# Weight decoding from groups of two chunks, and the first block's convolution in six pieces

## The chip, the cores and the metric

One core of a Trainium2 chip runs the whole kernel. The metric is the device time in microseconds (us). The engines are named as the profile names them: PE (TensorE; its weight loads are PEld), DVE (VectorE), ACT (ScalarE), POOL (GpSimd) and SP (SyncE, which issues the DMAs here).

## What is computed

```python
# x: (4, 4096, 192), weight_gen: (4, 4096, 8, 7); w_in: (192, 2048), w_out: (2048, 192)
w = softmax(weight_gen, axis=-1)                       # 7 weights per token and head
x_pad = concatenate([zeros((B, 6, D)), x], axis=1)
out[b, s, head h] = sum over k of w[b, s, h, k] * x_pad[b, s + k, head h]
h = out.reshape(16384, 192) @ w_in
g = where(h >= 1, h, where(h <= -1, 0, (h + 1)**2 / 4))
return (g @ w_out).astype(float32)
```

The two weight matrices arrive as 64-bit floats, because a float32 array is multiplied by a float64 scalar. The kernel turns them into 32-bit numbers itself; this is called decoding below.

## The kernel before

**Blocks and pairs.** The 16384 tokens are cut into 32 blocks of 512. For each block the 2048 hidden features are worked through in 16 steps of 128, two steps at a time: a pair. There are 8 pairs per block (NP) and 256 in all. A pair is 18 matmuls of the first product (`gemm1_pair`, L378, high and low parts of x and of the weights), then per step a relu pass, a square pass (ACT, L389 and L392), a min/max pass (DVE, L397, `act_g`), a high part (ACT, L403) and a low part (DVE, L404, `gl`), then 32 matmuls of the second product (`gemm2_part`, L432), which come two pairs later. The order of instructions on each engine is the order in which the code is written; each engine works its list in order.

**Decoding.** The weights come in 8 chunks (NCH) of two steps each; chunk c serves pair c. Part 0 of a chunk is its piece of w_in, part 1 its piece of w_out, each 128 partitions by 384 numbers. For each part a pass takes the top 16 bits of every 64-bit number into `head` (`cast_act` on ACT, L327; `cast_dve` on DVE, L331), a DVE pass joins them with the lower bits (`merge`, L340, two inputs in SBUF, result `psw` in a PSUM bank), and a high and a low part are written to `whi`/`wlo` or `wo` (`high` on ACT, L352; `low` on DVE, L356). All 64-bit numbers that a pass reads lie 8 bytes apart. Chunks 0 to 2 are decoded at the start and in `first_pairs`; chunk c = w + 1 is decoded during pair w in `early_pair`, for w = 2 to 6. From block 1 on no decoding is left.

**Block 0.** DVE and POOL form products of x with one of the 7 weights of the convolution, as pieces (`alone`, L227): one on DVE and three on POOL, and DVE adds three further products into a fifth (L244). PE turns each piece into the layout of the first product, four 128x128 turns for each third of the 192 features (`turn_sum`, L267, 60 turns in all), and sums the pieces in PSUM as it turns them. The last third also reads features 0 to 63 again, which `again` (ACT, L169) copies behind each piece. ACT and DVE then write the high and low parts `hc` and `hl` (L258, L259).

**Later blocks.** POOL does the whole convolution (L179 products, L189 sums). Block 1's result is turned on PE in pair 7 (`turn1`, `edge_pair`); from block 2 on DVE turns 32x32 squares (L284) and DMAs do the rest, and POOL writes the low parts `hl`. POOL's operations for block 1 wait by hand-made dependencies for the latest decoding pass of DVE (`gate`, `marks`). `ps_h` has 4 PSUM banks, shared by x, by decoded weights and by pairs.

**Loads.** SP issues them in this order: weight_gen, block 0's x, chunks 0, 1 and 2, block 1's x, chunk 3; the first chunk's load waits for a softmax pass of DVE. A chunk's rows are 1 KB (w_in) and 1.5 KB (w_out).

Of the kernel before, what the change touches and what calls it, by code (L numbers as in the profile page):

```python
# [22 lines left out]
def kernel(  # L23
# [21 lines left out]
    nc = tc.nc  # L45
# [38 lines left out]
    raw = ctx.enter_context(tc.tile_pool(name="raw", bufs=4))  # L84
# [131 lines left out]
    def conv_summed(b):  # L216
# [30 lines left out]
        return alone, wn, wt[:, gi], lambda: times(nc.vector, acc, wn, 1), add, own  # L247
# [4 lines left out]
    def split_x(b, src, engines):  # L252
# [8 lines left out]
        return ops  # L261

# [41 lines left out]
    def load_weights(c, behind=None):  # L304
        r = raw.tile([P, 4 * CN + 2], U16, tag="r", name="r")
        for h in range(2):
            f = c * CF + h
            load = nc.sync.dma_start(
                out=r[h * Q:(h + 1) * Q, 1:1 + 4 * C1].rearrange("q (k c) -> q k c", k=NC),
                in_=w_in[:, f * P:(f + 1) * P].rearrange("(k q) c -> q k c", q=Q).bitcast(U16))  # L310
            if behind is not None:
                tc.add_manual_dep(load.ins, behind.ins.name, SYNC, reason="the first block goes first")
                behind = None
# [18 lines left out]

    psw = {}

    def merge(c, part):
        word = raw_t[c].bitcast(U32)[:, 1:1 + 2 * CN].rearrange("p (c t) -> p c t", t=2)[:, :, 0]
# [423 lines left out]
```

## Time and profile before

| | |
|---|---|
| device time, 3 runs | median 1143.42 us (1143.4 to 1144.77) |
| span of the profiled execution | 1141.3 us (first to last instruction; no other time of that execution is given, so the median lies 2.1 us above the span) |
| PE busy | 1128.6 us (99%) |
| ACT, DVE, POOL busy | 964.6, 833.6, 792.3 us (85, 73, 69%) |
| granted PE clock | 1.000 over the span (the upper of the two levels) |
| DMA | 91.43 MB; busiest in the first 38 us |

Times are counted from the first instruction. A busy PE is not a PE at its peak, since matmuls are pipelined and their ends modelled: the count of matmuls in a stretch says more than the busy share.

### The profile page before, as it was taken

To read this page: it belongs to the slowest core of one execution; us is meant where nothing else is said; L and a number is where in the kernel's file an instruction comes from. 1 tells how busy PE (TensorE), PEld (TensorE's weight loads), DVE (VectorE), ACT (ScalarE), POOL (GpSimd) and SP (SyncE) were. 2 spreads that over 40 slices of the span, in tenths; PEclk is the share of its full clock that TensorE was granted. 3 is DMA by queue.
4 is the path that set the end of the run, shared out by engine and by line. 5 is a ranking of instruction groups with operands and counts; after the bars stand their busy time and mean duration, and the time that the engine had idled before them with its cause. 6 is when DMAs were issued, how large, how long until landed. Compare 5 with 4: busy or idle time off the path is not lost.

```text
span 1141.3 us, 32240 instructions
## 1 busy us (share of the span) xinstructions
PE 1128.6 (99%) x12885; PEld 1077.9 (94%) x12885; DVE 833.6 (73%) x1271; ACT 964.6 (85%) x1745; POOL 792.3 (69%) x511
## 2 busy tenths in 40 slices
PE   7999999999999999999999999999999999999998
PEld 5789999999999999999999999999999999999998
DVE  8877867777676777767777676776767777677765
ACT  6878888888888888888888888888888888888886
POOL 4799876777857678586686866678586785866310
PEclk9999999999999999999999999999999999999999
DMA  9422222222222212222122222222222122221100
GB/s 228 118 67 82 92 86 92 77 65 74 90 78 91 69 65 90 81 87 91 43 90 73 85 92 78 65 74 90 77 92 76 57 91 82 82 91 43 48 24 29
DMA packets 84053, 91.43 MB, mean 80 GB/s; under 512 B 5056, under 2 KB 75712, under 8 KB 83904
## 3 DMA queue, kind: packets, MB, share of 16 engines
q1 hardware_dynamic: 83904, 89.39, 24.7%
q8 instruction: 101, 1.65, 0.6%
q14 instruction: 48, 0.39, 0.1%
HBM read 64.99 MB, written 24.38 MB: 78 GB/s over the span
## 4 chain that ended last, share of the span: by engine, by line
PE 94%; ACT 3%; DVE 2%; issue 1%; DMA 0%; DVEq 0%; POOL 0%; POOLq 0%
PE o L432 47%; PE psh L378 46%; ACT u L392 1%; PE psx L267 1%; ACT gh L403 1%; DVE psh L397 1%; ACT u L389 1%; DMA x<-in_x_dram 0%; ACT whi L352 0%; DVE psw L340 0%; DVE gl L404 0%; ACT wo L352 0%; ACT osb L456 0%; DVE wo L356 0%; DVE piece L227 0%
## 5 line engine op out<-in xcount | busy, mean ns | idle before, releaser
L432 PE MATMUL o<-wo,gh 64*128 64x384 f32 x4096 | 645.5, 353 | 1.0 <-SPq L441 1.0
L432 PE MATMUL o<-wo,gl 64*128 64x192 f32 x4096 | 623.4, 247 | 0.0
L432 PEld LDWEIGHTS o<-wo,gh 64*128 64x128 f32 x4096 | 592.9, 184 | 6.5 <-SPq L441 1.2
L432 PEld LDWEIGHTS o<-wo,gl 64*128 64x128 f32 x4096 | 573.1, 187 | 0.1
L397 DVE SCALAR_TENSOR_TENSOR psh<-u,psh 128x512 f32<-128x512 f32 x512 | 354.4, 695 | 283.3 <-ACT u L392 282.9
L378 PE MATMUL psh<-hc,whi 64*128 64x512 f32 x1536 | 461.0, 395 | 4.2 <-DVE wlo L356 2.8
L378 PE MATMUL psh<-hc,wlo 64*128 64x512 f32 x1536 | 453.9, 389 | 0.0
L378 PE MATMUL psh<-hl,whi 64*128 64x512 f32 x1536 | 452.4, 388 | 0.0
L389 ACT ACTIVATE u<-psh 128x512 f32<-128x512 f32 x512 | 301.2, 588 | 78.2 <-PE psh L378 77.1
L404 DVE TENSOR_TENSOR gl<-psh,gh 128x512 fp32r<-128x512 f32 x512 | 345.5, 685 | 14.7 <-ACT gh L403 0.5
L403 ACT ACTIVATE gh<-psh 128x512 fp32r<-128x512 f32 x512 | 299.5, 592 | 63.4 <-DVE psh L397 63.4
L189 POOL TENSOR_TENSOR acc<-acc,pr 128x768 f32<-128x768 f32 x185 | 343.8, 1858 | 5.7 <-DVE head L331 2.0
L392 ACT ACTIVATE u<-u 128x512 f32<-128x512 f32 x512 | 324.3, 633 | 16.0
L378 PEld LDWEIGHTS psh<-hc,whi 64*128 64x128 f32 x1536 | 281.5, 184 | 19.3 <-DVE wlo L356 4.8
L378 PEld LDWEIGHTS psh<-hl,whi 64*128 64x128 f32 x1536 | 281.0, 184 | 15.7 <-DVE hl L259 0.3
L179 POOL TENSOR_TENSOR pr<-x,w 128x768 f32<-128x768 f32 x186 | 287.0, 1550 | 7.1 <-DVE psw L340 7.1
L378 PEld LDWEIGHTS psh<-hc,wlo 64*128 64x128 f32 x1536 | 282.0, 185 | 10.3
L259 POOL TENSOR_TENSOR hl<-XT,hc 128x512 fp32r<-128x512 f32 x90 | 115.6, 1297 | 206.9 <-PE o L432 151.6
L179 POOL TENSOR_TENSOR acc<-x,w 128x768 f32<-128x768 f32 x31 | 48.0, 1547 | 70.2 <-DVE w L155 68.3
L258 ACT ACTIVATE hc<-XT 128x512 fp32r<-128x512 f32 x90 | 55.5, 618 | 0.0
L284 DVE STREAM_TRANSPOSE T<-acc 128x768 f32<-128x768 f32 x30 | 50.0, 1665 | 0.0
L457 DVE SCALAR_TENSOR_TENSOR osb<-o,osb 128x384 f32<-128x384 f32 x64 | 32.5, 548 | 2.9 <-ACT osb L456 2.8
(44 smaller groups left out, 189.0 us busy)
## 6 DMA issues: line engine op xcount, KB each, us to landing
x<-in_x_dram SPq DMA_DIRECT2D x28, 960.0 KB, 4.8
XT<-D SPq DMA_DIRECT2D x180, 128.0 KB, 2.7
out_dram<-osb SPq DMA_DIRECT2D x31, 384.0 KB, 3.2
D<-T SPq DMA_DIRECT2D x30, 384.0 KB, 2.3
x<-in_x_dram SPq DMA_DIRECT2D x4, 945.0 KB
w<-in_weight_gen_dram SPq DMA_DIRECT2D x15, 224.0 KB, 2.6
r<-in_moe_w_in_dram SPq DMA_DIRECT2D x16, 192.0 KB, 7.1
r<-in_moe_w_out_dram SPq DMA_DIRECT2D x8, 384.0 KB, 12.3
```

The lines of the kernel that those rows point to most:

```text
L179: held(eng.tensor_tensor(out=t, in0=xtile[:, k:k + n, :].rearrange("p j (h g) -> p j h g", h=H), in1=wt[:, gi, :, :, k:k + 1].to_broadcast ...
L189: held(eng.tensor_tensor(out=o, in0=s, in1=t, op=ALU.add))
L258: ops.append(lambda c=c: nc.scalar.activation(out=hc[:, c], in_=src[c], func=AF.Copy))
L259: ops.append(lambda c=c: lows.append(engines[c].tensor_tensor(out=hl[:, c], in0=src[c], in1=hc[:, c].bitcast(F32), op=ALU.subtract)))
L284: lambda: nc.vector.transpose(out=T.rearrange("p b c j -> p b j c"), in_=acc.rearrange("p j (r b) -> p b j r", b=R)),
L378: nc.tensor.matmul(out=pair[h][:, 0:N], lhsT=l[rows, f // 2, (c + h) % NC if b < 2 else c], rhs=r[rows, c], start=(s == 0), stop=(s == len ...
L389: nc.scalar.activation(out=u_t[i], in_=h_t[i][:, 0:N], func=AF.Relu, scale=0.5 * UNIT, bias=0.5)
L392: nc.scalar.activation(out=u_t[i], in_=u_t[i], func=AF.Square, scale=UNIT ** -0.5)
L397: nc.vector.scalar_tensor_tensor(out=pv, in0=uv, scalar=1.0 / UNIT, in1=pv, op0=ALU.min, op1=ALU.max)
L403: nc.scalar.activation(out=gh[:, 0:N], in_=gv, func=AF.Copy)
L404: nc.vector.tensor_tensor(out=gl[:, 0:N], in0=gv, in1=gh[:, 0:N].bitcast(F32), op=ALU.subtract)
L432: mm = nc.tensor.matmul(out=o_t[b][turn][:, k, 0:cols], lhsT=g_t[i][l][rows, t * P:(t + 1) * P], rhs=wo[rows, f].rearrange("p s d -> p (s ...
```

## The change

Weights are loaded in groups of two chunks (rows of 2 and 3 KB). The two chunks of a group are the even and the odd columns of its part of w_in, and the even and odd rows of w_out. So a pass that reads part 0 of a chunk now finds its 64-bit numbers 16 bytes apart; in part 1 they stay 8 bytes apart. The load of the first group waits for nothing, and block 1's x is issued behind it. Block 0's convolution has six pieces: DVE makes two products alone and adds two into a third piece, POOL makes three. Each piece takes eight turns (48 in all), for two banks; the last third of `hc` is copied by ACT out of the two banks, 64 partitions each, and that of `hl` by POOL out of the other thirds. The same holds for block 1. Casts move between DVE, ACT and POOL, and `first_pairs` is in another order, with its end in `second_pair`.

```diff
-    raw = ctx.enter_context(tc.tile_pool(name="raw", bufs=4))
+    raw = ctx.enter_context(tc.tile_pool(name="raw", bufs=2))
...
-        return alone, wn, wt[:, gi], lambda: times(nc.vector, acc, wn, 1), add, own
+        return alone, wn, wt[:, gi], lambda: times(nc.vector, acc, wn, 2), add, own
...
+        def over(to, of, c):
+            nc.gpsimd.tensor_copy(out=hl[to, NC - 1], in_=hl[of, c])
+
+        return {
+            "hc0": lambda: high_of(hc[:, 0], src[0]), "hc1": lambda: high_of(hc[:, 1], src[1]),
+            "hcU": lambda: high_of(hc[upper, NC - 1], src[0][lower]),
+            "hcL": lambda: high_of(hc[lower, NC - 1], src[1][upper]),
+            "hl0": lambda: low_of(0), "hl1": lambda: low_of(1),
+            "hlU": lambda: over(upper, lower, 0), "hlL": lambda: over(lower, upper, 1)}
...
-            out=r[:, 1 + 4 * C1:1 + 4 * CN].rearrange("p (f c) -> p f c", f=CF),
-            in_=w_out[c * CF * P:(c + 1) * CF * P, :].rearrange("(f p) c -> p f c", p=P).bitcast(U16))
-        raw_t[c] = r
+            out=r[:, 1 + 8 * C1:1 + 8 * CN].rearrange("p (f c) -> p f c", f=CF),
+            in_=w_out[f0:f0 + 2 * CF * P, :].rearrange("(f p e) c -> p f (e c)", p=P, e=2).bitcast(U16))
+        raw_t[g] = r
+
+    def of_chunk(v, c, part):
+
+        if part == 0:
+            return v[:, 0:2 * C1].rearrange("p (k c e) -> p e k c", k=NC, e=2)[:, c % 2]
+        return v[:, 2 * C1:2 * CN].rearrange("p (f e d) -> p e f d", f=CF, e=2)[:, c % 2]
...
+        if w == 0:
+            passes = [p for p in passes if p[1] is hc] + [p for p in passes if p[1] is hl]
...
-        load_weights(0, marks[6])
+        load_weights(0)
+        load_x(1)
         load_weights(1)
-        load_weights(2)
-        load_x(1)
-        load_weights(3)
...
         cast_act(0, 0)
-        again(own[0])
-        pieces.append(own[0])
+        cast_act(1, 0)
+        cast_pool(0, 1)
...
         def first_pairs():
+            high(1, 0)
+            low(1, 0)
+            cast_act(1, 1)
             merge(0, 1)
             merge(1, 1)
...
+            wave(1)
+            load_weights(2)
+            gemm1_pair(1)
+            high(0, 1)
             relu(0)
...
+            cast_dve(2, 0)
             merge(2, 0)
...
+            wave(2)
...
+        def second_pair():
+            cast_dve(2, 1)
             split_g(2)
             split_g(3)
+            merge(2, 1)
+            high(2, 1)
             cast_act(3, 0)
+            low(2, 1)
             cast_dve(3, 1)
...
-            splits = split_x(1, src1, [nc.vector] * NC)
+            x1 = split_turned(1, src1)
...
-            turn1(2)
             gemm2_part(w - 1, 1)
             split_g(i)
+            x1["hcU"]()
+            x1["hcL"]()
+            x1["hlU"]()
+            x1["hlL"]()
```

DVE's list for block 0's sum, from the first piece to the first `merge`, before:

```order
L227 TENSOR_TENSOR piece_173<-x_111,near_154 128x4x192
L227 TENSOR_TENSOR sums_155<-x_111,near_154 128x768
L227 TENSOR_TENSOR tap_183<-x_111,near_154 128x768
L244 TENSOR_TENSOR sums_155<-sums_155,tap_183 128x768
L227 TENSOR_TENSOR tap_189<-x_111,near_154 128x768
L244 TENSOR_TENSOR piece_191<-sums_155,tap_189 128x4x192
L340 SCALAR_TENSOR_TENSOR psw_255<-r_135,head_99 128x384
```

and after the change:

```order
L224 TENSOR_TENSOR piece_164<-x_111,near_146 128x768
L224 TENSOR_TENSOR piece_168<-x_111,near_146 128x768
L224 TENSOR_TENSOR sums_147<-x_111,near_146 128x768
L224 TENSOR_TENSOR tap_175<-x_111,near_146 128x768
L240 TENSOR_TENSOR piece_177<-sums_147,tap_175 128x768
L369 SCALAR_TENSOR_TENSOR psw_230<-r_135,head_99 128x384
```

One of the two additions is gone, and the products go to two pieces instead of one.

DVE's list in the changed kernel from the two `merge` passes of w_out's chunks 0 and 1 to the last low part of pair 0 (`r_140` is the second group, `head_99` and `head_100` take even and odd chunks, `psh0_250` and `psh0_251` are pair 0):

```order
L369 SCALAR_TENSOR_TENSOR psw_273<-r_135,head_99 128x384
L369 SCALAR_TENSOR_TENSOR psw_275<-r_135,head_100 128x384
L386 TENSOR_TENSOR wo_98<-psw_273,wo_98 128x2x192
L356 TENSOR_SCALAR head_99<-r_140 128x384
L369 SCALAR_TENSOR_TENSOR psw_308<-r_140,head_99 128x384
L429 SCALAR_TENSOR_TENSOR psh0_250<-u_304,psh0_250 128x512
L386 TENSOR_TENSOR wlo_97<-psw_308,whi_96 128x384
L429 SCALAR_TENSOR_TENSOR psh0_251<-u_318,psh0_251 128x512
L386 TENSOR_TENSOR wo_98<-psw_275,wo_98 128x2x192
L436 TENSOR_TENSOR gl_325<-psh0_250,gh_324 128x512
L436 TENSOR_TENSOR gl_329<-psh0_251,gh_328 128x512
```

Chunk 2's first cast (the fourth row) stands on DVE right behind these merges and reads the second group; before, it stood on ACT, and both merges of chunk 2 came before the first min/max pass of pair 0. Now only one does.

POOL's list in the changed kernel around the end of block 1's convolution and the start of block 2's (`acc_788`):

```order
L186 TENSOR_TENSOR piece_249<-acc_277,pr_679 128x768
L176 TENSOR_TENSOR acc_788<-x_446,w_109 128x768
L176 TENSOR_TENSOR pr_790<-x_446,w_109 128x768
L273 COPY hl_841<-hl_841 64x512 x2
L176 TENSOR_TENSOR pr_920<-x_446,w_109 128x768
L186 TENSOR_TENSOR acc_788<-acc_788,pr_790 128x768
```

The two copies of `hl` are new in this list; they stand behind the second product of block 2, and the rest of that convolution stands behind them.

## Rows read from the trace of the kernel before

**Rows 1.** Busy time by stretch: us, each engine's busy (instructions), clock, DMA, GB/s.

```profile
12.80:28.20 15.40, 11.99 (x98) 9.03 (x98) 14.60 (x30) 12.47 (x25) 5.52 (x4) 1.00 1.09 253
28.20:50.20 22.00, 20.54 (x209) 17.24 (x208) 20.61 (x40) 19.18 (x39) 13.59 (x8) 1.00 0.66 155
80.60:1100.00 1019.40, 1019.40 (x11776) 983.58 (x11778) 740.20 (x1115) 875.67 (x1578) 736.28 (x469) 1.00 0.24 78
```

**Rows 2.** Timeline of block 0's start: start, duration, instruction, idle before and releaser.

```profile
7.20 0.95 DVE L227 TENSOR_TENSOR piece<-x,near 128x768 f32<-128x768 f32 x1 [0.28 <-DMA x<-in_x_dram]
8.21 6.77 PE L267 MATMUL psx<-ident,piece 128*128 128x128 f32 x60 [0.22 <-DVE piece L227]
14.14 1.58 ACT L258 ACTIVATE hc<-psx 128x512 fp32r<-128x512 f32 x3 [0.25 <-PE psx L267]
```

**Rows 3.** Timeline, DVE: the merges of chunks 3, 4 and 7.

```profile
28.19 1.03 DVE L340 SCALAR_TENSOR_TENSOR psw<-r,head 128x384 uint32<-128x384 uint32 x2
...
33.41 1.02 DVE L340 SCALAR_TENSOR_TENSOR psw<-r,head 128x384 uint32<-128x384 uint32 x2
...
49.09 1.02 DVE L340 SCALAR_TENSOR_TENSOR psw<-r,head 128x384 uint32<-128x384 uint32 x2
```

**Rows 4.** Page, groups of instructions: busy us, mean ns of one, idle before.

```profile
L404 DVE TENSOR_TENSOR gl<-psh,gh 128x512 fp32r<-128x512 f32 x512 | 345.5, 685 | 14.7 <-ACT gh L403 0.5
...
L389 ACT ACTIVATE u<-psh 128x512 f32<-128x512 f32 x512 | 301.2, 588 | 78.2 <-PE psh L378 77.1
...
L392 ACT ACTIVATE u<-u 128x512 f32<-128x512 f32 x512 | 324.3, 633 | 16.0
L403 ACT ACTIVATE gh<-psh 128x512 fp32r<-128x512 f32 x512 | 299.5, 592 | 63.4 <-DVE psh L397 63.4
```

**Rows 5.** Groups by line and form on DVE, first 140 us.

```profile
L340 DVE SCALAR_TENSOR_TENSOR psw<-r,head 128x384 uint32<-128x384 uint32 x16 | 8.2, 559 | 0.1
L284 DVE STREAM_TRANSPOSE T<-acc 128x768 f32<-128x768 f32 x3 | 5.0, 1670 | 0.0
L356 DVE TENSOR_TENSOR wlo<-psw,whi 128x384 fp32r<-128x384 f32 x8 | 4.4, 547 | 0.4
...
L331 DVE TENSOR_SCALAR head<-r 128x384 f16<-128x384 bf16 x7 | 2.7, 385 | 0.0
```

**Rows 6.** Timeline: one POOL operation and two DVE operations of the softmax.

```profile
4.57 0.97 POOL L150 TENSOR_TENSOR w<-w,m 128x448 f32<-128x448 f32 x1 [1.88 <-DVE m L149]
...
4.81 0.77 DVE L153 TENSOR_SCALAR s<-s 128x32 f32<-128x32 f32 x1
...
13.54 0.19 DVE L153 TENSOR_SCALAR s<-s 128x64 f32<-128x64 f32 x1
```

**Rows 7.** DMA by stretch: us, PE clock, DMA share, GB/s.

```profile
8.00:17.00 9.00, 1.00 1.09 217
17.00:20.00 3.00, 1.00 1.04 403
```

**Rows 8.** Groups by line and form on POOL, first 140 us.

```profile
L179 POOL TENSOR_TENSOR pr<-x,w 128x768 f32<-128x768 f32 x27 | 41.6, 1548 | 7.1 <-DVE psw L340 7.1
...
L259 POOL TENSOR_TENSOR hl<-XT,hc 128x512 fp32r<-128x512 f32 x6 | 7.7, 1292 | 3.2 <-DMA XT<-D 2.4 <-ACT hc L258 0.8
...
L543 POOL CAST ident<-ident 128x128 bf16<-128x128 f32 x1 | 0.3, 289 | 0.1
```

**Rows 9.** Timeline: the end of block 2's convolution on POOL, and DVE.

```profile
72.08 3.77 POOL L189 TENSOR_TENSOR acc<-acc,pr 128x768 f32<-128x768 f32 x2
...
75.06 0.85 DVE L153 TENSOR_SCALAR s<-s 128x64 f32<-128x64 f32 x1
...
76.41 1.58 DVE L284 STREAM_TRANSPOSE T<-acc 128x768 f32<-128x768 f32 x1
```

**Rows 10.** The chain that ended last, around the start of pair 13.

```profile
79.85 0.69 DVE gl L404
...
80.59 2.28 PE psh L378 x17
```

More of the change, by code (lines that the diff above doesn't have):

```diff
@@ L302, with load_weights, by_piece @@
     raw_t, marks = {}, []
-    def load_weights(c, behind=None):
-        r = raw.tile([P, 4 * CN + 2], U16, tag="r", name="r")
+    def load_weights(g):
+        r = raw.tile([P, 8 * CN + 2], U16, tag="r", name="r")
+        f0 = g * 2 * CF * P
         for h in range(2):
[L307 to L313, printed above, removed]
-        nc.sync.dma_start(
-            out=r[:, 1 + 4 * C1:1 + 4 * CN].rearrange("p (f c) -> p f c", f=CF),
-            in_=w_out[c * CF * P:(c + 1) * CF * P, :].rearrange("(f p) c -> p f c", p=P).bitcast(U16))
-        raw_t[c] = r
+            nc.sync.dma_start(
+                out=r[h * Q:(h + 1) * Q, 1:1 + 8 * C1].rearrange("q (k c) -> q k c", k=NC),
+                in_=w_in[:, f0 + h * 2 * P:f0 + (h + 1) * 2 * P].rearrange("(k q) c -> q k c", q=Q).bitcast(U16))
+        nc.sync.dma_start(
+            out=r[:, 1 + 8 * C1:1 + 8 * CN].rearrange("p (f c) -> p f c", f=CF),
[5 more added lines that the diff above has]
+        return v[:, 2 * C1:2 * CN].rearrange("p (f e d) -> p e f d", f=CF, e=2)[:, c % 2]
+    def by_piece(v, part):
+        return v.rearrange("p (k c) -> p k c", k=(NC, CF)[part])
     def tops(c, part):
-        sl = (slice(0, C1), slice(C1, CN), slice(0, CN))[part]
-        top = raw_t[c][:, 2:2 + 4 * CN].rearrange("p (c t) -> p c t", t=4)[:, sl, 2]
-        return heads[c % 2][:, sl, 1].bitcast(F16), top.bitcast(BF16)
+        sl = (slice(0, C1), slice(C1, CN))[part]
+        top = raw_t[c // 2][:, 2:2 + 8 * CN].rearrange("p (c t) -> p c t", t=4)[:, :, 2]
+        return by_piece(heads[c % 2][:, sl, 1], part).bitcast(F16), of_chunk(top, c, part).bitcast(BF16)
     def cast_act(c, part):
@@ L589, in first_pairs @@
         def first_pairs():
+            high(1, 0)
+            low(1, 0)
+            cast_act(1, 1)
             merge(0, 1)
             merge(1, 1)
-            tc.add_manual_dep(s1[6]().ins, marks[-1].ins.name, SYNC, reason="the decoding of a chunk goes first")
-            load_weights(4)
-            load_weights(5)
+            wave(1)
+            load_weights(2)
+            gemm1_pair(1)
+            high(0, 1)
             relu(0)
-            high(1, 0)
-            low(1, 0)
-            gemm1_pair(1)
-            cast_act(2, 0)
-            high(0, 1)
-            high(1, 1)
             low(0, 1)
-            low(1, 1)
-            cast_dve(2, 1)
+            cast_dve(2, 0)
             merge(2, 0)
-            merge(2, 1)
-            wave(3)
-            load_weights(6)
+            wave(2)
             square(0)
-            relu(1)
             high(2, 0)
-            high(2, 1)
-            square(1)
             act_g(0)
             low(2, 0)
-            low(2, 1)
+            relu(1)
+            square(1)
+            high(1, 1)
             act_g(1)
+            low(1, 1)
             split_g(0)
+            split_g(1)
             relu(2)
             square(2)
-            split_g(1)
             relu(3)
@@ L701 @@
                 elif 1 < w < NP - 1:
+                    if w == 2:
+                        second_pair()
                     early_pair(w)
```

63 lines of the change are left out of this document (39 added, 24 removed).

## The prediction

> **What bounds the kernel now.** I read the busy time by stretch first. From 80.6 us on PE issues 11.6 matmuls per us without a gap [rows 1]; nothing the change touches lies there, so it can only move the moment at which that stretch begins. Ahead of it two stretches are bound by DVE, not by PE: from 12.8 to 28.2 us DVE is busy 14.60 of 15.40 us, and from 28.2 to 50.2 us 20.61 of 22.00, while PE issues only 9.5 matmuls per us [rows 1]. In the second stretch each pair takes one turn of a loop (merge on DVE, high parts, relu and square on ACT, min/max and low parts on DVE): from the merge of chunk 3 to that of chunk 7 there are four turns in 49.09 - 28.19 = 20.9 us, 5.22 us each [rows 3]. After 50 us the chain of work goes through DVE once more: POOL's last sum for block 2 ends at 75.85, DVE's small softmax pass ends with it at 75.91, its 32x32 turn follows at 76.41 [rows 9], and pair 13 starts at 80.59 just behind a low part that DVE wrote from 79.85 on [rows 10]. So three places count: when the merge of chunk 3 starts (28.19), how long a turn of the loop takes, and when POOL ends block 2's sum.
>
> **1. The start, up to the merge of chunk 3.** DVE loses one addition of 768 (a product of that size takes 0.95 [rows 2]), one low part of 512 (0.69 [rows 4]) and two casts, one of them of double width; it gains one cast of 0.39 [rows 5]: about 2.2 us less work. The turns fall from 60 to 48. They are back to back at 6.77 / 60 = 0.113 us now [rows 2], so the sums would be complete near 13.2 instead of 14.1: DVE's third piece is ready at 7.20 + 4 x 0.87 + 0.96 = 11.6, POOL's at 11.8, and 16 turns are left for these two. Behind that ACT makes four copies of 0.53 (1.58 for three now [rows 2]), to 15.3; DVE's low parts and the two w_out merges end near 17.3, one more low part near 17.8, and there the cast of chunk 2 can begin, its merge at 18.1. From this merge to that of chunk 3 the order after the change is a chain that passes from DVE to ACT and back: merge 0.56, then ten passes of ACT in a row (two high parts of weights at 0.53 as a copy of `hc` takes, three relus of 0.59, two high parts `gh` of 0.59, three squares of 0.63; 5.9 together), then on DVE min/max 0.69, cast 0.39, two low parts of 0.69, merge 0.56, on ACT a high part, on DVE low part 0.55 and cast 0.39 [rows 4, 5]. By durations that is 11 us; where passes of one engine follow each other the next starts about 0.09 before the last is written out (two merges of 0.56 take 1.03 [rows 3]), some eleven times, so 10.0 us. The merge of chunk 3 comes at 18.1 + 10.0 = 28.1, against 28.19 now [rows 3]: **-0.1**. DVE's saved work is spent waiting for ACT, because half of chunk 2's decoding now stands behind the passes of pairs 0 and 1. The four extra copies and casts on ACT lie ahead of this chain, beside PE's turns; without that cover they would cost their 0.5 each.
>
> **2. What can be late at 17.8.** The first product of block 1 on POOL is released by the last of the two w_out merges, at 17.3, and runs 1.55 [rows 8], to about 18.9. DVE's cast arrives at 17.8. A small DVE pass that met a POOL operation took 0.77 and ended with it, where it takes 0.19 alone [rows 6]. So the cast would end near 19.1 instead of 18.1: **+1.0**. Before the change POOL's products are released only after both merges of chunk 2. The Trainium skill, SBUF — State Buffer, section Who interferes with whom, says that such a DVE pass and a GpSimd operation share one pair of ports under an exclusive lock, so that the second waits for the whole of the first; the rows agree, and by the rule the sum is the same.
> The weights could be later still. Ahead of chunk 2's w_in lie one group (1.57 MB), block 1's x (0.98) and 0.79 MB, from about 6.1 us on, when block 0's x is through. Weights in small rows move at 217 GB/s, x in 7.7 KB rows at 403 [rows 7]: at these rates 7.2 + 2.4 + 3.6 us and about 1 us to land give 20.4, and if rows of 2 and 3 KB moved like x, 15.5. Between them, nearer the middle, the load hides under the collision; at the late end the cast ends at 20.7, 1.6 more. Bounds for this place: 0 to +2.6.
>
> **3. Reading at 16 bytes.** No pass before reads SBUF in this pattern with two inputs. The nearest row is DVE's 32x32 turn, which reads 24 bytes apart and writes 16 apart: 1.67 us for 768 numbers [rows 5], against 0.95 for a plain product of 768 [rows 2]; that is 0.94 ns more per number, or 0.36 us for 384. The other bound is 0: at 8 bytes a merge takes 0.56, like a low part of the same size that reads dense [rows 5]. The turn may owe its time to being a turn; I take 0.36 for a merge of part 0, since it is the only row with such steps. It stands once in the chain of point 1: **+0.4**. In the loop it stands in five turns, chunks 3 to 7, where DVE has 0.06 of its time free [rows 1]: 5 x 0.36 = **+1.8**. ACT's cast of part 0 I leave at its 0.64; if it paid the same it would add up to 0.3 in four turns (0 to +1.2). The Trainium skill, SBUF — State Buffer, section Specifications (TRN2), says that SBUF lines are 16 bytes and that full bandwidth needs at least two hits in a line; 8 bytes apart gives two, 16 apart gives one. It speaks against this change; a halved rate (one more cycle per number, an estimate from its clock of 0.96 GHz) would be 0.4 per merge and 2.4 in all, against 2.2 here.
>
> **4. Block 1's edge and POOL.** PE loses four turns, 0.45 us. ACT's two half copies lie in its wait for pair 8 and cost nothing there. POOL gains two copies of 64x512 in front of block 2's third product. Bounds: 0.29 (a cast of 128 numbers) and 1.29 (a low part of 512 with two inputs) [rows 8]; I take 0.7, since a copy has one input of those two and four times the numbers of the cast. What stands behind the copies on POOL moves with them, so its sum for block 2 ends 1.4 later, at 77.25, and DVE's turn starts at 77.4 instead of 76.41 [rows 9]; pair 13 waits for what stands behind it on DVE [rows 10]: **+1.0**. PE's 0.45 is swallowed by this wait. With copies of 0.29 the wait is gone and 0.45 is gained; with 1.29 it is +2.1.
>
> **Sum.** -0.1 + 1.0 + 0.4 + 1.8 + 1.0 = +4.1 us. The span would be 1145.4, and with the 2.1 us that the median has over the span now, **1147.5 us**.
>
> **Rivals.** *No cost of 16 bytes*: points 1, 2 and 4 alone, +1.9, 1145.3. For it: reading at 8 bytes costs DVE nothing. *The saved work comes through (faster)*: the merge of chunk 3 is led by DVE, not by ACT, as it is now with 14.60 of 15.40 us busy [rows 1]; then its 2.2 us are gained, the turns give 0.45, and with POOL copies near 0.3 and no cost of 16 bytes nothing is given back: -2.6, 1140.8. It decides for this that the merge of chunk 3 starts before 26.5 us. Against it: the chain of point 1 has ten ACT passes in a row. *The second group lands late*: the load of point 2 at its slow end, +1.6 on top, 1149.1; the larger rows would then have brought nothing, so that the change would not do what it does on paper. For it: the DMA queue is full all the time (1.09) [rows 7].
>
> **How the numbers follow.** Chances: the forecast 0.38, no cost of 16 bytes 0.27, saved work 0.25, late group 0.10. About 0.2%, 2.3 us, is what a measurement of this kernel can tell from no change. The forecast (+4.1) and the late group (+5.7) are slower, 0.48; no cost of 16 bytes (+1.9) is within it, 0.27; the saved work is faster, 0.25. The forecast's own range is 1145.5 to 1149, from its bounds at points 3 and 4. A range of 1140.8 to 1149.0 leaves out half of the saved-work case (0.12) and most of the late group (0.07).
>
> **What would show it.** The merges of part 0 at 0.9 and those of part 1 at 0.56; the cast of chunk 2 drawn out to the end of a POOL product; the merge of chunk 3 at 29 to 30 us and that of chunk 7 some 22.3 us behind it; DVE's turn for block 2 behind POOL's sum. Wrong it would be if all merges take 0.56, if the merge of chunk 3 starts before 28 us, or if POOL's copies are short enough to vanish in front of the turn.

## The result, and the profile after

The changed kernel takes 1152.26 us (median of 4 runs, 1152.0 to 1152.7) where the kernel before takes 1143.51 (4 runs, 1143.4 to 1144.77): a ratio of 1.0074, 95% interval 1.006 to 1.0089. It is slower, as forecast, but by 8.7 us instead of 4.1, and outside the range (1140.8 to 1149.0). The span of the profiled execution is 1150.1 us, 8.8 above that of before.

Busy time by stretch, the changed kernel (columns and stretches as in [rows 1]):

```profile
12.80:28.20 15.40, 11.05 (x72) 7.91 (x72) 12.77 (x21) 11.64 (x21) 8.79 (x8) 0.89 0.98 250
28.20:50.20 22.00, 17.71 (x174) 15.21 (x174) 19.65 (x36) 18.11 (x34) 10.18 (x6) 0.92 0.47 131
80.60:1100.00 1019.40, 1018.26 (x11751) 1014.60 (x11749) 740.73 (x1116) 872.67 (x1572) 741.30 (x472) 1.00 0.24 78
```

In the first stretch DVE issues 21 instructions instead of 30 and is busy 12.77 us instead of 14.60, and PE issues 72 matmuls instead of 98: both wait more. The long stretch is nearly what it was (11751 matmuls against 11776, about 2 us at 11.6 per us), so most of the time is lost ahead of it. Where, the timeline shows (rows of DVE, PE, ACT and POOL in order of time):

```profile
8.57 1.82 DVE L224 TENSOR_TENSOR piece<-x,near 128x768 f32<-128x768 f32 x2 [1.76 <-DMA x<-in_x_dram]
9.58 5.55 PE L286 MATMUL psx<-ident,piece 128*128 128x128 f32 x48 [1.13 <-DVE piece L224]
12.72 1.74 ACT L352 ACTIVATE head<-r 128x384 f16<-128x384 bf16 x2 [6.04 <-DMA r<-in_moe_w_in_dram]
13.67 0.88 DVE L369 SCALAR_TENSOR_TENSOR psw<-r,head 128x384 uint32<-128x384 uint32 x1 [0.57 <-ACT head L352]
14.97 0.59 ACT L267 ACTIVATE hc<-psx 128x512 fp32r<-128x512 f32 x1
15.86 0.68 DVE L270 TENSOR_TENSOR hl<-psx,hc 128x512 fp32r<-128x512 f32 x1
16.57 1.83 ACT L267 ACTIVATE hc<-psx 64x512 fp32r<-64x512 f32 x3 [1.01 <-DVE hl L270]
18.44 0.69 DVE L270 TENSOR_TENSOR hl<-psx,hc 128x512 fp32r<-128x512 f32 x1 [1.14 <-ACT hc L267]
19.51 1.18 DVE L369 SCALAR_TENSOR_TENSOR psw<-r,head 128x384 uint32<-128x384 uint32 x2
20.83 1.54 POOL L176 TENSOR_TENSOR acc<-x,w 128x768 f32<-128x768 f32 x1 [1.02 <-issue]
21.31 1.43 DVE L356 TENSOR_SCALAR head<-r 128x384 f16<-128x384 bf16 x1
22.77 0.85 DVE L369 SCALAR_TENSOR_TENSOR psw<-r,head 128x384 uint32<-128x384 uint32 x1
31.07 0.56 DVE L369 SCALAR_TENSOR_TENSOR psw<-r,head 128x384 uint32<-128x384 uint32 x1
32.97 1.31 DVE L369 SCALAR_TENSOR_TENSOR psw<-r,head 128x384 uint32<-128x384 uint32 x2
38.68 1.32 DVE L369 SCALAR_TENSOR_TENSOR psw<-r,head 128x384 uint32<-128x384 uint32 x2
42.83 1.45 DVE L436 TENSOR_TENSOR gl<-psh,gh 128x512 fp32r<-128x512 f32 x2
43.45 0.90 ACT L352 ACTIVATE head<-r 128x384 f16<-128x384 bf16 x1
44.38 1.32 DVE L369 SCALAR_TENSOR_TENSOR psw<-r,head 128x384 uint32<-128x384 uint32 x2
55.80 1.32 DVE L369 SCALAR_TENSOR_TENSOR psw<-r,head 128x384 uint32<-128x384 uint32 x2
64.09 1.28 POOL L273 CAST hl<-hl 64x512 fp32r<-64x512 f32 x2
80.57 3.81 POOL L186 TENSOR_TENSOR acc<-acc,pr 128x768 f32<-128x768 f32 x2
84.41 1.66 DVE L303 STREAM_TRANSPOSE T<-acc 128x768 f32<-128x768 f32 x1 [1.32 <-POOL acc L186]
```

Read from the top: block 0's x lands for a first product at 8.57 and PE's turns start at 9.58 (7.20 and 8.21 before [rows 2]). The cast of chunk 0 waits for the first group until 12.72, and two casts of 0.87 stand ahead of the first copy `hc0`, which starts at 14.97 (14.14 before [rows 2]). ACT's half copies wait 1.01 us for DVE's first low part, then DVE's second low part 1.14 us for ACT's last half copy. Chunk 2's cast (L356) starts at 21.31 behind POOL's product and is drawn out to 1.43. The merge of chunk 3 is at 32.97 (28.19 before), that of chunk 7 at 55.80 (49.09 before [rows 3]). DVE's turn for block 2 waits for POOL's sum and starts at 84.41 (76.41 before [rows 9]).

How late the changed kernel is at each place, by the starts of the merges and of min/max passes (`act_g`):

| place | before | after | later by |
|---|---|---|---|
| merge of chunk 3 | 28.19 | 32.97 | 4.78 |
| min/max, pair 6, first step | 51.19 | 58.19 | 7.00 |
| min/max, pair 10, first step | 71.94 | 78.55 | 6.61 |
| min/max, pair 11, first step | 77.89 | 85.94 | 8.05 |
| min/max, pair 14, first step | 88.83 | 96.91 | 8.08 |
| end of the span | 1141.3 | 1150.1 | 8.8 |

So the loss has three parts: 4.8 us at the start (forecast 1.3), 2.2 in the loop (forecast 1.8), 1.1 at block 2's sum (forecast 1.0), and 0.7 that comes later.

### The profile page after: what moved, and what is told of

Read it like the earlier page. It is cut to its first block, busy times and chain, and to the rows that moved or that the text cites. A ratio compares the mean times of both kernels' runs of the same rounds, so it can differ in the third digit from the quotient of the medians.

```text
span 1150.1 us, 32194 instructions
## 1 busy us (share of the span) xinstructions
PE 1130.7 (98%) x12869; PEld 1112.9 (97%) x12869; DVE 836.3 (73%) x1267; ACT 967.5 (84%) x1742; POOL 796.5 (69%) x516
## 4 chain that ended last, share of the span: by engine, by line
PE 92%; ACT 3%; DVE 2%; POOL 1%; DMA 1%; issue 0%; SPq 0%; DVEq 0%; POOLq 0%; ACTq 0%
PE psh L410 46%; PE o L464 45%; DMA r<-in_moe_w_in_dram 1%; ACT u L424 1%; POOL acc L186 1%; DVE psw L369 1%; ACT u L421 1%; DVE psh L429 0%; POOL pr L176 0%; ACT gh L435 0%; DMA XT<-D 0%; ACT head L352 0%; DVE gl L436 0%; ACT wo L382 0%; ACT whi L382 0%
## 5 line engine op out<-in xcount | busy, mean ns | idle before, releaser
L464 PE MATMUL o<-wo,gh 64*128 64x384 f32 x4096 | 625.8, 353 | 0.6 <-SPq L473 0.6
L464 PE MATMUL o<-wo,gl 64*128 64x192 f32 x4096 | 604.0, 247 | 0.0
L464 PEld LDWEIGHTS o<-wo,gl 64*128 64x128 f32 x4096 | 582.1, 187 | 0.2
L410 PE MATMUL psh<-hc,whi 64*128 64x512 f32 x1536 | 403.2, 397 | 10.7 <-DVE wlo L386 6.9
L410 PE MATMUL psh<-hc,wlo 64*128 64x512 f32 x1536 | 396.2, 390 | 0.0
L410 PE MATMUL psh<-hl,whi 64*128 64x512 f32 x1536 | 394.6, 390 | 0.0
L436 DVE TENSOR_TENSOR gl<-psh,gh 128x512 fp32r<-128x512 f32 x512 | 345.3, 685 | 15.3 <-ACT gh L435 0.7
L410 PEld LDWEIGHTS psh<-hc,whi 64*128 64x128 f32 x1536 | 235.6, 185 | 18.1 <-DVE wlo L386 8.2
L410 PEld LDWEIGHTS psh<-hl,whi 64*128 64x128 f32 x1536 | 235.7, 185 | 2.8
L410 PEld LDWEIGHTS psh<-hc,wlo 64*128 64x128 f32 x1536 | 235.6, 186 | 1.9 <-DVE wlo L386 0.2
```

What stands on the lines that cost most here:

```text
L410: nc.tensor.matmul(out=pair[h][:, 0:N], lhsT=l[rows, f // 2, (c + h) % NC if b < 2 else c], rhs=r[rows, c], start=(s == 0), stop=(s == len ...
L436: nc.vector.tensor_tensor(out=gl[:, 0:N], in0=gv, in1=gh[:, 0:N].bitcast(F32), op=ALU.subtract)
L464: mm = nc.tensor.matmul(out=o_t[b][turn][:, k, 0:cols], lhsT=g_t[i][l][rows, t * P:(t + 1) * P], rhs=wo[rows, f].rearrange("p s d -> p (s ...
```

## The experiments

All times are medians of device time, beside the kernel before on the same chip (its medians were 1143.47 to 1143.97).

**1. Block 0's x first.** The load of the first group waits as the first chunk's load did before:

```diff
-        load_weights(0)
+        load_weights(0, marks[6])
```

> The changed kernel, but the load of the first weight group waits for the softmax pass of DVE, as the first chunk's load did before. Theory 1 (the first copy hc0 starts late, at 14.97 us, because ACT has two casts of 0.9 us in front of it and these wait for the first group, which lands at 12.72): x of block 0 lands near 7.1 instead of 8.6 and DVE's first product starts 1.4 us earlier, but the group lands no sooner, hc0 starts at 15 us or later, and the time stays at 1152 us or rises by up to 1 us. Rival (the late x of block 0 costs it): hc0 starts 1.4 us earlier, merge of chunk 3 at 31.6, and the time is 1150.9 us.

1151.67 us (1150.9 to 1152.28); ratio 1.0067, interval 1.005 to 1.0084. The timeline of this run:

```profile
7.79 1.82 DVE L224 TENSOR_TENSOR piece<-x,near 128x768 f32<-128x768 f32 x2
13.39 1.71 ACT L355 ACTIVATE head<-r 128x384 f16<-128x384 bf16 x2 [5.68 <-DMA r<-in_moe_w_in_dram]
15.62 0.59 ACT L267 ACTIVATE hc<-psx 128x512 fp32r<-128x512 f32 x1
22.16 0.98 DVE L359 TENSOR_SCALAR head<-r 128x384 f16<-128x384 bf16 x1 [0.43 <-DMA r<-in_moe_w_in_dram]
```

x comes 0.8 us sooner, but the group, issued later, lands at 13.39 instead of 12.72, and `hc0` starts later than without this edit. As theory 1 expected, the first group's arrival sets `hc0` here. That the late x costs nothing in the changed kernel is not shown, since this edit moves both loads. The last row is a second finding: chunk 2's cast now waits for the second group.

**2. No shared bank.** ACT makes the third part of `hc` out of SBUF instead of the PSUM banks that DVE reads for `hl`:

```diff
-            "hcU": lambda: high_of(hc[upper, NC - 1], src[0][lower]),
-            "hcL": lambda: high_of(hc[lower, NC - 1], src[1][upper]),
+            "hcU": lambda: high_of(hc[upper, NC - 1], hc[lower, 0].bitcast(F32)),
+            "hcL": lambda: high_of(hc[lower, NC - 1], hc[upper, 1].bitcast(F32)),
```

> The changed kernel, but the two half copies of the third part of hc read hc's first and second part in SBUF instead of the PSUM banks, so that ACT and DVE no longer read one bank at the same time. Theory 1 (ACT's first half copy waited 1.01 us for DVE's first low part, and DVE's second low part waited 1.14 us for ACT's second half copy, because both read the same bank): both waits are gone, the two merges of w_out start 1.1 to 1.3 us earlier (18.3 instead of 19.51), the merge of chunk 3 at 31.8 instead of 32.97, the time is 1151.0 us. Rival (the second group of weights, not DVE, holds chunk 2's cast): that cast stays at 21.3 us or moves by less than 0.5, and the time stays within 0.5 us of 1152.3.

1149.99 us (1149.34 to 1151.18); ratio 1.0054, interval 1.0039 to 1.0069. The timeline:

```profile
14.48 0.60 ACT L267 ACTIVATE hc<-psx 128x512 fp32r<-128x512 f32 x1
16.72 0.67 DVE L270 TENSOR_TENSOR hl<-psx,hc 128x512 fp32r<-128x512 f32 x1
17.90 1.06 DVE L369 SCALAR_TENSOR_TENSOR psw<-r,head 128x384 uint32<-128x384 uint32 x2
20.81 0.51 DVE L356 TENSOR_SCALAR head<-r 128x384 f16<-128x384 bf16 x1 [1.21 <-DMA r<-in_moe_w_in_dram]
```

Both waits are gone; the w_out merges start 17.90 - 14.48 = 3.42 us behind `hc0`, against 19.51 - 14.97 = 4.54 in the changed kernel: 1.12 us. But the cast then waits 1.21 us for the second group, which lands only at 20.8. So both theories hold a part: the bank waits are real, and right behind them the load is the next bound. The time fell by 2.3 us, more than the 1.3 that theory 1 expected; in the profiled execution `hc0` also came 0.49 earlier, and POOL's product had ended (at 20.64) when the cast began, so that the cast took 0.51.

**3. POOL's product later.** It is released by the merge of chunk 2's w_in:

```diff
             merge(1, 1)
-            wave(1)
...
             merge(2, 0)
-            wave(2)
+            wave(3)
```

> The changed kernel, but POOL's first product of block 1 is released by the merge of chunk 2's w_in, together with the next two, instead of by the second w_out merge. Theory 1 (chunk 2's cast on DVE took 1.43 us instead of 0.39 because it met that product on POOL): the cast takes 0.39, the merge of chunk 3 starts near 31.9 instead of 32.97, and the time is 1151.2 us. Rival (what follows the cast waits for ACT or for the weights anyway): the cast is short but the merge of chunk 3 stays at 32.9 and the time at 1152.3 us.

1150.34 us (1149.89 to 1151.56); ratio 1.0058, interval 1.0043 to 1.0073. The timeline:

```profile
20.68 0.52 DVE L356 TENSOR_SCALAR head<-r 128x384 f16<-128x384 bf16 x1 [0.30 <-DMA r<-in_moe_w_in_dram]
21.23 0.84 DVE L369 SCALAR_TENSOR_TENSOR psw<-r,head 128x384 uint32<-128x384 uint32 x1
```

The cast falls from 1.43 to 0.52: theory 1. In this run too it waited for the second group, until 20.68. Counted from `hc0` (at 14.26 here, 0.71 earlier than in the changed kernel) the merge of chunk 2 comes 6.97 us later instead of 7.80, so the edit is worth 0.8 us in this execution; most of the rest of the fall is the earlier start.

**4. Eight bytes.** The two chunks of a group are contiguous halves of it:

```diff
-        return v[:, 0:2 * C1].rearrange("p (k c e) -> p e k c", k=NC, e=2)[:, c % 2]
+        return v[:, 0:2 * C1].rearrange("p (k e c) -> p e k c", k=NC, e=2)[:, c % 2]
...
-            in_=w_out[f0:f0 + 2 * CF * P, :].rearrange("(f p e) c -> p f (e c)", p=P, e=2).bitcast(U16))
+            in_=w_out[f0:f0 + 2 * CF * P, :].rearrange("(f p) c -> p f c", p=P).bitcast(U16))
```

> The changed kernel, but the two chunks of a group are the two contiguous halves of its columns of w_in and of its rows of w_out: all 64-bit numbers are read 8 bytes apart again; w_in's rows stay at 2 KB, w_out's fall back to 1.5 KB. Theory 1 (a merge of part 0 costs 0.3 us more and ACT's cast 0.26 more at 16 bytes): merges of part 0 take 0.56, a turn of the loop falls from 5.71 to about 5.25, five turns give 2.3 us, the start 0.5, and the time is 1149.5 us. Rival (the loop's longer turn comes from the order of the passes, not from the distance): turns stay above 5.5 us and the time above 1151.5 us.

1150.74 us (1148.19 to 1152.28); ratio 1.0057, interval 1.0039 to 1.0076. The timeline, rows of PE and DVE:

```profile
9.75 7.13 PE L286 MATMUL psx<-ident,piece 128*128 128x128 f32 x48 [1.98 <-DVE piece L224]
33.35 1.03 DVE L369 SCALAR_TENSOR_TENSOR psw<-r,head 128x384 uint32<-128x384 uint32 x2
38.57 1.03 DVE L369 SCALAR_TENSOR_TENSOR psw<-r,head 128x384 uint32<-128x384 uint32 x2
```

A turn of the loop takes 38.57 - 33.35 = 5.22 us, as before the change, against 5.71, and two merges 1.03 against 1.31: theory 1. The median falls by 1.5 us only; the four executions spread over 4 us, so it says little. The profiled one (1149.4 us) lost time at its start, which the edit does not explain: its 48 turns took 7.13 us, where they take 5.55 in the changed kernel; PE had stood idle for 1.98 us ahead of them, and the granted clock was low (busy time by stretch, PE, clock, DMA share, GB/s):

```profile
10.00:12.00 2.00, 2.00 (x13) 0.59 1.03 200
```

Chunk 2's cast is worth a look in this run: it ran beside POOL's product (22.08 to 23.63) and took 0.59 us only, from 22.51 on; the merge behind it, which has two inputs in SBUF, took 0.91. So a POOL product does not draw out every such cast.

**5. ACT makes the copies.** Block 1's two copies of `hl` go to ACT:

```diff
         def over(to, of, c):
-            nc.gpsimd.tensor_copy(out=hl[to, NC - 1], in_=hl[of, c])
+            if b:
+                nc.scalar.activation(out=hl[to, NC - 1], in_=hl[of, c].bitcast(F32), func=AF.Copy)
+            else:
+                nc.gpsimd.tensor_copy(out=hl[to, NC - 1], in_=hl[of, c])
```

> The changed kernel, but the two copies that make block 1's third part of hl are ACT's, not POOL's. Theory 1 (they cost POOL 1.28 us in front of block 2's sum, and with it DVE's 32x32 turn and pair 11 wait): everything up to pair 10 stands as in the changed kernel, POOL's sum for block 2 and DVE's turn come 1.3 us earlier, and the time is 1151.0 us. Rival (DVE's turn waits for something else, or ACT's copies delay pair 8 by as much): pair 11 starts within 0.3 us of the changed kernel and the time stays at 1152.0 or more.

1151.31 us (1149.49 to 1156.42); ratio 1.0073, interval 1.0056 to 1.0089: too wide to tell 1 us. The profile tells it. Its start was 1.2 us later than the changed kernel's (again 7.13 us for the turns), so the path ahead is compared by steps: from pair 10 to pair 11 the lateness against before goes from 8.52 to 8.28, where in the changed kernel it goes from 6.61 to 8.05. DVE's turn follows the pass ahead of it without a wait:

```profile
80.32 3.77 POOL L186 TENSOR_TENSOR acc<-acc,pr 128x768 f32<-128x768 f32 x2
84.66 1.62 DVE L306 STREAM_TRANSPOSE T<-acc 128x768 f32<-128x768 f32 x1
```

That is theory 1 in the mechanism. The rival has a share: with ACT's copies in front of pair 8, PE's saved turns are no longer gained there (the lateness grows from 8.24 at pair 6 to 8.52, where it fell from 7.00 to 6.61).

**6 to 8. Edits put together.** Run 6 has run 2's edit and block 1's x behind the second group:

```diff
         load_weights(0)
-        load_x(1)
         load_weights(1)
+        load_x(1)
```

> The changed kernel with hc's half copies out of SBUF (as in the run without the shared banks), and block 1's x issued behind the second weight group instead of ahead of it. Theory 1 (with the bank waits gone chunk 2's cast waits for the second group, which lands at 20.7 us because 0.97 MB of x stand in front of it): the cast starts when DVE is through, near 19.6, its merge near 20.1 instead of 21.35, the merge of chunk 3 near 30.3 instead of 31.55, and the time is 1148.8 us. Rival (the load's own rate or its issue holds it, not its place): the cast stays at 20.5 us or later and the time at 1150 us.

1150.64 us (1149.54 to 1151.86); ratio 1.006, interval 1.0047 to 1.0073. The timeline:

```profile
9.43 1.82 DVE L224 TENSOR_TENSOR piece<-x,near 128x768 f32<-128x768 f32 x2 [1.47 <-DMA x<-in_x_dram]
17.17 0.60 ACT L267 ACTIVATE hc<-psx 128x512 fp32r<-128x512 f32 x1 [1.17 <-PE psx L286]
22.29 0.52 DVE L356 TENSOR_SCALAR head<-r 128x384 f16<-128x384 bf16 x1
25.03 1.54 POOL L176 TENSOR_TENSOR acc<-x,w 128x768 f32<-128x768 f32 x1 [4.19 <-DMA x<-in_x_dram]
```

The cast no longer waits for the load; it starts 22.29 - 17.17 = 5.12 us behind `hc0`, against 6.33 in run 2. But `hc0` itself came at 17.17 here (x late, slow turns), so the time shows nothing of it: inconclusive on the time. The last row shows the price of the new order: POOL's first product of block 1 waits for x until 25.03. Run 7 adds the eight bytes of run 4:

> The kernel of the run before with the 64-bit numbers 8 bytes apart as well. Theory 1 (16 bytes cost 0.3 us per merge and 0.26 per cast, and these lie on the path in every turn of the loop): a turn of the loop takes 5.22 us instead of 5.71, merges of part 0 take 0.56, and the time is 2.3 to 2.9 us below that run's, near 1146.2 us. Rival (the loop's turn is as long at 8 bytes once the start is faster): less than 1 us below it.

1147.71 us (1147.53 to 1150.2); ratio 1.0042, interval 1.003 to 1.0054: 2.9 below run 6, as theory 1 expected, but partly by luck. `hc0` came at 14.32 instead of 17.17, and of the 3.4 us between the two profiled spans 2.35 are there at the merge of chunk 3 (30.68 against 33.03). Behind it the four turns of the loop take 21.64 us against 22.88, so 8 bytes gave 1.2 us there. Run 8 adds ACT's copies of run 5:

> The kernel with hc's half copies out of SBUF, block 1's x behind the second group and 8 bytes, and block 1's two copies of hl on ACT as well. Theory 1 (POOL's two copies delay block 2's sum by 1.28 us, which DVE's turn and pair 11 wait for): 1.0 us below the run without the last edit, near 1146.7 us. Rival (PE's wait behind pair 11 is as long, since ACT's copies delay pair 8 instead): within 0.4 us of 1147.7.

1146.9 us (1145.83 to 1149.25); ratio 1.0026, interval 1.0016 to 1.0037: 0.8 below run 7, but on another chip; the excess over the kernel before falls from 4.2 to 2.9 us, and the two intervals overlap, so the time alone does not decide. The profile speaks for theory 1: the lateness from pair 10 to 11 goes from 3.84 to 3.62 here, in run 7 from 2.86 to 4.30.

**9 and 10. The first group chunk by chunk.** Run 9: run 8, but the first group waits as in run 1 and is loaded in 1 KB rows, chunk 0's w_in first, into the same interleaved places; ACT's cast of chunk 1 stands behind its first half copy (only this last part of the edit is shown):

```diff
         cast_act(0, 0)
-        cast_act(1, 0)
...
         x0["hcU"]()
+        cast_act(1, 0)
         merge(1, 0)
```

> The kernel of the run before, but the first group's load waits for the softmax pass again and comes chunk by chunk (1 KB rows, chunk 0's w_in first), and ACT's cast of chunk 1 stands behind its first half copy. Theory 1 (chunk 0's cast waits for the whole group's w_in, twice the bytes, until 12 to 13.7 us, and the early load delays x of block 0; this sets hc0): hc0 starts near 13.5 us as with the convolution alone, against 14.3 to 17.2 in the runs with the group, the merge of chunk 3 near 29, the time is 1144.5 us, with a spread under 1 us. Rival (the order of the decoding passes holds the merge of chunk 3 whatever comes first): the merge stays at 30 us or later and the time above 1146 us.

1149.48 us (1149.31 to 1150.56); ratio 1.005, interval 1.0037 to 1.0063. The merge of chunk 3 is at 33.26 and the time above 1146 us, as the rival has it, but the run tests neither theory. The timeline's row says why:

```profile
14.31 0.63 ACT L373 ACTIVATE head<-r 128x384 f16<-128x384 bf16 x1 [7.35 <-DMA r<-in_moe_w_in_dram]
```

The first cast waited until 14.31 all the same, so the early chunk was not had. I took the interleaved places for the reason, which no run isolates, and gave each chunk of the first group its own in run 10 (places that follow one another, and block 1's x between the second group's w_in and w_out; the loads themselves are left out of the cut):

```diff
+        if c < 2:
+            w = (hi - lo) // 2
+            return v[:, lo + c * w:lo + (c + 1) * w].rearrange("p (k c) -> p k c", k=(NC, CF)[part])
...
-        load_weights(0)
-        load_weights(1)
-        load_x(1)
+        load_weights(0, marks[6])
+        load_weights(1, None, lambda: load_x(1))
```

> The kernel of the last but one run (SBUF half copies, 8 bytes, ACT's copies of hl), with the first group's two chunks in places of their own, loaded chunk by chunk (1 KB rows) behind the softmax pass, the second group's w_in next, then block 1's x, then that group's w_out; ACT's cast of chunk 1 stands behind its first half copy. In the run before, chunk 0's and chunk 1's numbers lay interleaved in one place and the cast waited until 14.31 us. Theory 1 (with a group chunk 0's cast waits for both chunks' bytes, and this sets hc0): chunk 0's cast starts before 12.2 us, hc0 near 13.5, the merge of chunk 3 near 29.5 instead of 31.7, the time is 1144.8 us. Rival (the order of the passes or the second group's arrival holds the merge of chunk 3): hc0 is early, but the merge of chunk 3 stays at 31 us or later and the time at 1146.3 us or more.

1146.1 us (1144.97 to 1146.94); ratio 1.0021, interval 1.0012 to 1.003. The timeline:

```profile
8.57 5.55 PE L289 MATMUL psx<-ident,piece 128*128 128x128 f32 x48 [1.41 <-DVE piece L224]
10.52 0.65 ACT L377 ACTIVATE head<-r 128x384 f16<-128x384 bf16 x1 [3.72 <-DMA r<-in_moe_w_in_dram]
13.72 0.60 ACT L267 ACTIVATE hc<-psx 128x512 fp32r<-128x512 f32 x1 [0.62 <-PE psx L289]
19.83 0.57 DVE L394 SCALAR_TENSOR_TENSOR psw<-r,head 128x384 uint32<-128x384 uint32 x1
29.69 1.03 DVE L394 SCALAR_TENSOR_TENSOR psw<-r,head 128x384 uint32<-128x384 uint32 x2
```

The first cast starts at 10.52 instead of 12.72, `hc0` now waits for PE and not for weights, and the merge of chunk 3 comes at 29.69: theory 1 at each place, though the median fell by 0.8 us instead of 2 and so lies at the rival's time (the profiled execution, 1145.1 us, is one of the fastest of the ten). What stays is the chain: the merge of chunk 2 is earlier than before the change (19.83 against 20.52), the merge of chunk 3 still 1.5 later, since the way from the one to the other takes 9.9 us instead of 7.7.

**11 and 12. The convolution alone.** Run 11 is the kernel before with its loads and its order of decoding, and only the convolution of the change (half copies out of SBUF as in run 2, block 1's copies on ACT):

```diff
-        run(split_x(0, src, [nc.vector] * NC))
+        x0 = split_turned(0, src)
+        for part in ("hc0", "hcU", "hc1", "hcL", "hl0", "hl1", "hlU", "hlL"):
+            x0[part]()
```

> The kernel of before with its loads, its decoding and its order of decoding; only the convolution of the change (six pieces, eight turns each), with hc's third part copied by ACT out of SBUF and hl's third part copied by POOL for block 0 and by ACT for block 1. Theory 1 (the convolution's saved DVE work is worth its 1.0 to 1.6 us where DVE leads the start, and the change lost it to its loads and its order): the merge of chunk 3 starts near 27.0 instead of 28.19 and the time is 1142.2 us. Rival (the saved work is spent waiting whatever the order is, since the weights' arrival sets the start): the merge of chunk 3 stays between 27.9 and 28.5 and the time between 1143.0 and 1144.0 us.

1143.67 us (1143.24 to 1144.3); ratio 1.0, interval 0.9992 to 1.0009: no difference. The timeline, ACT and DVE:

```profile
13.45 0.60 ACT L267 ACTIVATE hc<-psx 128x512 fp32r<-128x512 f32 x1 [0.62 <-PE psx L289]
17.63 0.60 ACT L411 ACTIVATE u<-psh 128x512 f32<-128x512 f32 x1 [1.64 <-PE psh L400]
18.64 0.56 DVE L378 TENSOR_TENSOR wlo<-psw,whi 128x384 fp32r<-128x384 f32 x1 [0.24 <-ACT whi L374]
28.51 1.03 DVE L362 SCALAR_TENSOR_TENSOR psw<-r,head 128x384 uint32<-128x384 uint32 x2
```

`hc0` starts 0.7 us earlier than before and the merge of chunk 3 0.3 later: the saved work turns into DVE's waits for ACT (0.41 and 0.59 us for `hc`, 0.24 in the third row), and ACT's relu waits for PE nearly as long as before (1.64 us against 1.73). The rival holds for the time. Run 12 moves the passes that made those waits:

```diff
-        for part in ("hc0", "hcU", "hc1", "hcL", "hl0", "hl1", "hlU", "hlL"):
+        for part in ("hc0", "hc1", "hcU", "hcL", "hl0", "hl1", "hlU", "hlL"):
...
-            relu(0)
             high(1, 0)
             low(1, 0)
+            relu(0)
```

> The kernel of before with the convolution of the change (as in the run with that part alone), but ACT writes both full parts of hc ahead of the two half copies, and chunk 1's high part ahead of pair 0's relu. Theory 1 (the DVE work that the convolution saves was spent waiting for ACT, which made hc's second part late and held chunk 1's high part behind a relu that waits for PE): both waits go, the merge of chunk 3 starts near 27.7 instead of 28.51, the time is 1142.8 us. Rival (the wait only moves to the next pass, since ACT, DVE and PE pass the work round in a chain): the merge of chunk 3 stays above 28.2 us and the time between 1143.2 and 1144.0.

1144.7 us (1142.88 to 1144.84); ratio 1.0003, interval 0.9994 to 1.0012: no difference. In the profiled execution, the slowest of the eleven, the loads came late (DVE's first product at 7.96, 0.7 us later than in run 11, the first cast 1.0 later), and DVE then waited 0.68 us for chunk 1's weights:

```profile
16.71 0.61 DVE L353 TENSOR_SCALAR head<-r 128x768 f16<-128x768 bf16 x1 [0.68 <-DMA r<-in_moe_w_out_dram]
28.83 1.04 DVE L362 SCALAR_TENSOR_TENSOR psw<-r,head 128x384 uint32<-128x384 uint32 x2
```

The interval leaves out theory 1's time (1142.8 us, a ratio of 0.9992), and the rival's time, 1143.2 to 1144.0, was missed too. The mechanism is not decided: the merge of chunk 3 is 0.3 us later than in run 11, but counted from `hc0` (14.12 against 13.45) it is 0.35 earlier, and DVE's wait for the weights may belong to this late start alone. No version tried beats the kernel before.

## Why the prediction was right and wrong

**Point 1 failed, at its start.** Its sum had `hc0` at 13.2, ACT's copies done at 15.3, the cast of chunk 2 at 17.8. They came at 14.97, 18.40 and 21.31. Of the 8.8 us in the span 4.1 were forecast; of the 4.7 missing these 3.5 are the most (0.4 is the loop's, 0.7 comes after pair 14). Two steps made 3.1 of the 3.5 us; the other 0.4 is DVE's way from the last copy to the cast, 2.9 us instead of 2.5.
- "the sums would be complete near 13.2", from the turns alone: nothing in it prices the load that waits for nothing, nor the wait for a group of two chunks. (Its own terms, 11.6 and 16 turns of 0.113, give 13.4.) `hc0` came 1.8 us later than forecast, and either of the two would have done it nearly alone. The late x: in runs 10 to 12, where `hc0` waits for PE, it starts 5.15 to 5.16 us behind PE's first turn, which in the changed kernel puts it at 9.58 + 5.16 = 14.74. The group: chunk 0's cast could start at 12.72 only, two casts stood ahead of `hc0`, and that put it at 14.97. In runs 2, 3 and 7, with the group whole, `hc0` stands 5.15 to 5.17 behind the first turn, just where x lets it; in run 1, with x earlier and the group later, it came at 15.62; with x early and chunk 0 ahead (run 10), at 13.72.
- "Behind that ACT makes four copies of 0.53": they were put back to back beside DVE's low parts. They took 3.43 us from `hc0` to the end of the last one, instead of 2.1, because ACT's half copies and DVE's low parts read the same two banks and went one after the other (1.01 and 1.14 us of wait, each ended by the other engine's pass, 1.12 of it on the path by run 2); a copy also took 0.6 us instead of 0.53. Before the change the third part had a bank of its own, and ACT's three copies ran in 1.58 [rows 2]. The Trainium skill, PSUM — Partial Sum Buffer, section PSUM bank collisions raise a hardware error, says that two engines may not touch one bank (in the same group of 32 partitions) at once, reads against reads included, and that the program must put a wait between them. The trace agrees with its 1.01 and 1.14; this rule spoke against the change and I did not weigh it.

**The rest of point 1 was right.** From the merge of chunk 2 to that of chunk 3 the forecast was 10.4 us (10.0 and one merge at 16 bytes); it took 32.97 - 22.77 = 10.2. This is what remains when all else is undone: 9.9 in run 10, where runs 11 and 12, with the old loads and all or nearly all of the old order, take 7.7 as before the change. That it comes from half of chunk 2's decoding standing behind the passes of pairs 0 and 1 is argued from the lists; no run moved that half alone. The rival "the saved work comes through" asked for a merge of chunk 3 before 26.5; in runs 11 and 12 it comes at 28.51 and 28.83, so the saved work is not gained even there.

**Point 2.** The cast met POOL's product and took 1.43, 1.04 over a free one of 0.39 [rows 5] (forecast 1.0; run 3 undoes it). It ended 0.37 us behind the product (22.74 against 22.37), so nearly all of it ran behind that. In run 4, with 8 bytes, the same cast beside the product took 0.59; so the forecast held for this layout, and what decides is not shown. The load was worse than its late end: the second group lands near 20.7 (runs 2 and 3), not between 15.5 and 20.4. In the changed kernel this is hidden, because DVE arrives at 21.31. The two lie side by side, so undoing one alone uncovers the other: the rival "the second group lands late" was nearly as strong as the bound that came true.

**Point 3 was right in kind and a little small.** A merge of part 0 takes 0.85 instead of 0.56, 0.29 more (forecast 0.36). ACT's cast, left at its 0.64, takes 0.90, and this came into the path: DVE's low parts `gl` end at 44.28, ACT's cast at 44.35, the merge starts at 44.38. A turn of the loop takes 5.71 instead of 5.22, 0.48 more, and five turns cost 7.00 - 4.78 = 2.2 us instead of 1.8. Run 4 gives all of it back (four turns in 20.89 us, 20.90 before), run 7 all but 0.74, which it loses while PE's clock is low (last section). In the chain of point 1 the forecast was 0.4, and runs 8 and 10 show 0.35 (10.2 to 9.85). The estimate of 0.4 per merge that the prediction worked out from the Trainium skill (SBUF — State Buffer, section Specifications (TRN2)) was too high; the measurement decides for 0.29.

**Point 4 was right.** POOL's two copies took 1.28 (forecast 1.4). Up to pair 10 the lateness fell by 0.4 us, which I put down to PE's four turns (no run takes them alone), and the wait for POOL's sum took 1.4 at pair 11: 8.05 - 7.00 = 1.05, forecast 1.0. Runs 5 and 8 undo that wait.

**The signs.** Four of those that the prediction named came: the merges at 0.85 and 0.56, the drawn-out cast, 22.83 us from the merge of chunk 3 to that of chunk 7, and DVE's turn behind POOL's sum. The merge of chunk 3 at 29 to 30 us did not (32.97); it is the one that the start decides.

**Open.** From pair 14 on another 0.7 us is lost (8.08 to 8.8). A step of 0.97 stands at one place, the second step of pair 22 (9.23 later than before, the first step 8.26), where ACT waits 0.85 us for block 3's `XT` from a DMA. Some of it comes back behind that. It wasn't tried by itself. The runs of the kernels with the grouped load spread by up to 7 us, those of the kernel before by up to 3.4. In the eight profiles where the first group waits for nothing, DVE's first product starts at 8.1 to 9.4 us, in the six where the first weights wait at 7.2 to 8.0; what decides it within each set was not settled. Slow turns like those of run 4 (6.95 to 7.13 us) stand in runs 4, 5, 6 and 8.

## What to carry to other kernels

When a change shares one buffer between passes of two engines that had one each, write down who reads it at the same time: the shared read is a wait, and it stands on no list of instructions. When loads are grouped, price the first consumer: it waits for the whole group (the first cast at 12.72 us, at 10.52 with its own chunk ahead), and what other loads are under way beside it may come later (here x, by 1.4 us). Work saved on the engine that looks busiest was worth nothing here, where three engines pass one piece round: follow the next start of the loop's leading pass, not the busy share.

## What the runs showed of the hardware that I had not expected

The larger rows of w_in showed no gain in rate. Busy time by stretch of the changed kernel (us, PE, clock, DMA share, GB/s; the row names no load, so which one it was is inferred): from 16 to 18 us, where by the order of issue the second group's w_in with its 2 KB rows is under way, it is 192 GB/s, where 1 KB and 1.5 KB rows together made 217 before [rows 7]; from 12 to 14 us, with w_out's rows and then x, it is 422.

```profile
12.00:14.00 2.00, 2.00 (x20) 1.00 1.06 422
16.00:18.00 2.00, 0.66 (x6) 1.00 1.04 192
36.00:38.00 2.00, 2.00 (x12) 0.50 0.99 217
```

The last row shows PE at the lower of its two clock levels (1.2 GHz) after it had stood idle for 3.85 us from 31.1 on; it cost nothing there, since that turn of the loop takes 5.71 like the others. The clock was at this level for part of 18 to 20 us (0.65) and from 20 to 22 us (0.50) too, after PE had idled for 1.34 us up to 17.84; no pass of ACT or DVE waited for PE there. In run 7, where the loop's turn is short, it did: the granted clock was 0.50 from 32 to 38 us, ACT's relu waited 0.91 us for PE, and that turn took 5.83 instead of 5.22, the next 5.36.
